# Attention with a soft mixture of experts on one core: whole PSUM tiles for the products with v and the dispatch, ordered readers, and four sets of due numbers

## The chip, the cores and the metric

The kernel runs on one core of one Trainium2 chip. The metric is the device time of one execution in microseconds. The kernel before was timed in three runs: median 568.11 us, from 567.79 to 571.41. The profile is of a further execution.

## What is computed

Everything is float32. There are 8 batches with 8 heads, 576 tokens and a head size of 64. The first half is attention in which only the scores within tau of the row's maximum count; its result, with the heads of a token joined to 512 numbers, goes into a soft mixture of 8 experts with 4 slots each.

```python
scores = q @ k.T / 8
scores = where(scores >= max(scores) - tau, scores, -1e9)
attn = softmax(scores)                     # over the keys
x = join_heads(attn @ v)                   # 4608 x 512
logits = x @ phi                           # 4608 x 32
d = softmax(logits, axis=0)                # dispatch: over all tokens
slot_in = d.T @ x                          # 32 x 512
slot_out[e] = relu(slot_in[e] @ w1[e]) @ w2[e]
out = softmax(logits, axis=1) @ slot_out   # combine: over the slots
```

## The kernel before

**Pairs.** The work goes in 32 pairs of heads, four to a batch (`pair(p)`, L449; `j` is the pair's place in its batch, 0 to 3). The two heads of a pair lie on the two halves of the 128 partitions. A pair has nine row tiles `i` of 128 queries (the ninth holds the 64 queries left over of each head). Per row tile:
- TensorE multiplies q by k (`qk`, L494; the matmuls are L497, those of the ninth tile L502) into a PSUM tile;
- VectorE copies the negated scores to SBUF (`ss`) and takes the row's extreme in the same instruction (`nmx`, L509);
- ScalarE makes the exponentials `p` (L519), GpSimd the threshold `thr` (L522);
- VectorE masks `p` by the threshold and sums the row (L525).

After two row tiles TensorE transposes their `p` by 64 x 64 blocks (`ptr`, L418, matmuls at L424) and ScalarE copies the result out of PSUM (`act_copy`, L428, copies at L429) to `pTa` (the first 256 queries of a head), `pTb` (the other 320) or `pTl` (the left-over keys). For the ninth tile, the left-over rows `pL` are transposed at once with some left-over keys, and four copies read that one PSUM tile: one to `pTl`, one of 512 elements to `pTb` (L594), two of 64 partitions to `pTl` (L597). In the last pair the copy to `pTb` runs on VectorE (L433), else on ScalarE.

When the pair's rows are there, two products with v follow (L601 to L616; matmuls L612): 20 matmuls over `pTa` for 256 queries, 20 over `pTb` for 320, each into a PSUM tile of its own and copied to `xT`. Then `xT` is transposed to `x`; GpSimd scales `x` by the reciprocal sums (L627), and TensorE and ScalarE turn it back to `xT` (L632, L635; the operations called "new" in the plan).

**The dispatch.** After the fourth pair of a batch, `dispatch(b)` (L669) transposes the left-over columns (`xl`), multiplies `xT` by phi into the tile `wl` (the logits, L690), which then has three readers: VectorE's reduction to `M` (L695), ScalarE's exponential `dT` (L702), which needs the running extreme that a second small reduction makes of `M` (L698), and ScalarE's copy `l` of the logits for later (L429). `f` (L700) is the factor by which the sums so far are rescaled. `dT` and `l` are transposed; then `weigh` (L730) sums `ones` and `x` with the weights into `csum` and `acc` (L737 and L742, taken over by VectorE at L748 or L750). After the eighth batch ("end") the same runs with nothing beside it, followed by the slots' input.

**PSUM.** PSUM is four tiles of 128 x 2 x 512 float32, called regions (L31, L269). A buffer of kind "s" takes a whole region. A buffer of kind "w" takes one of its two halves of 512: a half of a region that is half used if there is one, else of an empty region (`take`, L185). Of kind "w" are the products with v, the logits and the two results of `weigh`, except in the last pair and the last batch, and three small uses at the start and the end:

```python
bank_of = lambda alone: Buf("s" if alone else "w")          # L412
w = bank_of(p == NP - 1)                                    # L604, products with v
wl = bank_of(b == B - 1)                                    # L684, logits
w = bank_of(b == B - 1)                                     # L733, weigh
```

**The order of the work.** Operations are not issued as they are written: each is added to a plan (`Order.add`, L135) with its engine, an assumed duration, what it reads and writes, and a due number. The due number is the pair's base (9 per pair) and an entry of `TABLE` (L41) under the operation's scope and its place in it: "first" and "last" for those pairs, "pair" for the 30 others, "batch" and "end" for the dispatches, "new", "soft" and so on. `plan` (L160) plays the operations through with the assumed durations: whenever an engine is free it takes, among its operations whose inputs are there and whose buffers have room, the one with the smallest due number. The order that comes out, and the buffers given, are then written down for each engine as they stand (`run`, L265); the waits between engines are put in when the kernel is built, from the tiles that the instructions touch. Loads by SyncE are in the plan too. In `add`, an operation depends on the writers of what it reads, and on the writers and the readers of what it writes (L144 to L148); two that only read the same thing are not ordered.

After the last batch come the experts and the combine (L870 to L1040), in an order written by hand, with eight PSUM tiles of their own.

## Time and profile before

| | us |
|---|---|
| median of three runs | 568.11 |
| lowest, highest run | 567.79, 571.41 |
| the profiled execution's own time | 567.51 |
| its span, first to last instruction | 565.7 |
| TensorE busy | 535.9 |
| VectorE busy | 468.8 |
| ScalarE busy | 458.0 |
| GpSimd busy | 251.6 |

The mean granted TensorE clock was 0.988 of full speed. In the profile, PE is TensorE's matmuls, PEld its weight loads, DVE is VectorE, ACT ScalarE, POOL GpSimd, SP SyncE. A row of the timeline gives the start, the length, the engine, the line, the operation, output and inputs, and a count where neighbours are merged; in square brackets stands how long the engine had been idle, and whose end released it. A row of waits names who waited for whom, with the total, the times and the longest. In a name such as `ps` the number of the buffer is left out, so the four regions are all `ps`. A line of the kernel can be a helper's: all transposes by `ptr` are L424 and all of ScalarE's copies by `act_copy` L429. Matmuls are pipelined and their ends are modelled.

### The profile page before, as it was taken

To read this page: it belongs to the slowest core of one execution; us is meant where nothing else is said; L and a number is where in the kernel's file an instruction comes from. 1 tells how busy PE (TensorE), PEld (TensorE's weight loads), DVE (VectorE), ACT (ScalarE), POOL (GpSimd) and SP (SyncE) were. 2 spreads that over 40 slices of the span, in tenths; PEclk is the share of its full clock that TensorE was granted. 3 is DMA by queue.
4 is the path that set the end of the run, shared out by engine and by line. 5 is a ranking of instruction groups with operands and counts; after the bars stand their busy time and mean duration, and the time that the engine had idled before them with its cause. 6 is when DMAs were issued, how large, how long until landed. Compare 5 with 4: busy or idle time off the path is not lost.

```text
span 565.7 us, 18326 instructions
## 1 busy us (share of the span) xinstructions
PE 535.9 (95%) x7022; PEld 346.4 (61%) x7022; DVE 468.8 (83%) x1327; ACT 458.0 (81%) x789; POOL 251.6 (44%) x478
## 2 busy tenths in 40 slices
PE   8999999999899999999899989998999998899991
PEld 6666666666566665666566656665666665553470
DVE  6999997999699979998899979996999899321192
ACT  4899998999799979999799979997999799412171
POOL 2465553555355544555355525553555556221030
PEclk9999999999999999999999999999999999899996
DMA  6255555555555552333033313333333413979488
GB/s 176 66 162 163 162 170 153 163 162 162 161 159 164 164 163 73 101 83 94 16 94 105 93 46 89 87 89 87 89 87 88 126 61 94 370 286 404 190 346 322
DMA packets 31990, 83.03 MB, mean 147 GB/s; under 512 B 4640, under 2 KB 12832, under 8 KB 31904
## 3 DMA queue, kind: packets, MB, share of 16 engines
q1 hardware_dynamic: 31904, 81.87, 46.8%
q8 instruction: 55, 0.90, 0.7%
q14 instruction: 31, 0.25, 0.1%
HBM read 72.42 MB, written 9.44 MB: 145 GB/s over the span
## 4 chain that ended last, share of the span: by engine, by line
PE 71%; ACT 17%; DVE 5%; issue 4%; SPq 1%; DMA 0%; DVEq 0%; POOL 0%; ACTq 0%; POOLq 0%
PE ps L612 25%; PE ps L497 19%; PE ps L424 14%; ACT p L519 6%; ACT pTa L429 3%; PE h L914 2%; PE ps L502 2%; ACT pTb L429 2%; PE so L948 2%; PE ps L632 1%; PE ps L737 1%; DVE ss L509 1%; ACT xT L429 1%; DVE cT L906 1%; ACT pL L519 1%
## 5 line engine op out<-in xcount | busy, mean ns | idle before, releaser
L509 DVE TENSOR_SCALAR_CACHE_REDUCE ss<-ps 128x576 f32<-128x576 f32 x288 | 208.0, 754 | 12.5 <-ACT pTl L429 8.9
L522 POOL TENSOR_SCALAR thr<-nmx,pabs 128x1 f32<-128x1 f32 x288 | 120.5, 419 | 199.7 <-DVE ss L509 190.1
L525 DVE SCALAR_TENSOR_TENSOR p<-ss,thr,p 128x576 f32<-128x576 f32 x256 | 201.4, 811 | 9.5 <-ACT p L519 9.0
L519 ACT ACTIVATE p<-ss,nmx 128x576 f32<-128x576 f32 x256 | 186.5, 778 | 18.9 <-DVE ss L509 18.7
L497 PE MATMUL ps<-k,q 64*128 64x288 f32 x1024 | 165.9, 427 | 6.4 <-ACT xT L429 4.9
L497 PEld LDWEIGHTS ps<-k,q 64*128 64x128 f32 x1024 | 85.0, 188 | 32.5 <-ACT pTb L429 14.0
L424 PE MATMUL ps<-ident,p 64*128 64x64 f32 x2304 | 100.8, 225 | 2.8 <-ACT pTa L429 1.5
L424 PEld LDWEIGHTS ps<-ident,p 64*128 64x128 f32 x2304 | 87.5, 140 | 19.1 <-ACT pTa L429 6.4
L429 ACT COPY pTb<-ps 128x1024 f32<-128x1024 f32 (+1 forms) x95 | 79.9, 872 | 2.3 <-PE ps L424 1.5
L612 PE MATMUL ps<-pTb,vv 128*64 128x320 f32 x512 | 75.9, 438 | 0.1
L429 ACT COPY pTa<-ps 128x1024 f32<-128x1024 f32 x64 | 65.7, 1028 | 0.4 <-PE ps L424 0.4
L612 PE MATMUL ps<-pTa,vv 128*64 128x256 f32 x512 | 62.9, 388 | 0.0
L612 PEld LDWEIGHTS ps<-pTb,vv 128*64 128x64 f32 x512 | 34.0, 136 | 36.0 <-issue 10.0
L612 PEld LDWEIGHTS ps<-pTa,vv 128*64 128x64 f32 x512 | 34.2, 138 | 26.1 <-DVE ss L509 9.0
L556 POOL TENSOR_SCALAR pL<-pL,ri 128x576 f32<-128x576 f32 x31 | 34.9, 1126 | 27.7 <-DVE ri L552 25.6
L612 PE MATMUL ps<-pTl,vv 128*64 128x256 f32 (+1 forms) x256 | 41.9, 406 | 0.0
L627 POOL TENSOR_TENSOR x<-x,ri 128x512 f32<-128x512 f32 x31 | 33.2, 1072 | 1.6 <-ACT x L429 1.6
L429 ACT COPY pTl<-ps 128x256 f32<-128x256 f32 x64 | 24.0, 376 | 5.2 <-PE ps L424 3.0
L429 ACT COPY xT<-ps 128x256 f32<-128x256 f32 (+1 forms) x63 | 24.6, 390 | 3.1 <-PE ps L612 3.1
L525 DVE SCALAR_TENSOR_TENSOR pL<-ss,thr,pL 128x576 f32<-128x576 f32 x32 | 26.5, 828 | 0.0
L879 POOL TENSOR_TENSOR c<-lall,crow 128x512 f32<-128x512 f32 x9 | 9.3, 1043 | 38.7 <-PE ct L416 38.7
L612 PEld LDWEIGHTS ps<-pTl,vv 128*64 128x64 f32 x256 | 18.4, 137 | 12.7
(137 smaller groups left out, 561.7 us busy)
## 6 DMA issues: line engine op xcount, KB each, us to landing
w<-in_w SPq DMA_DIRECT2D x44, 512.0 KB, 7.0
q<-in_qT SPq DMA_DIRECT2D x62, 288.0 KB, 4.5
vv<-in_vt SPq DMA_DIRECT2D x32, 320.0 KB, 4.6
host<-in_w SPq DMA_DIRECT2D x20, 512.0 KB, 6.7
k<-in_kT SPq DMA_DIRECT2D x62, 144.0 KB, 3.0
out<-w SPq DMA_DIRECT2D x8, 512.0 KB, 3.3
out<-host SPq DMA_DIRECT2D x8, 512.0 KB, 5.0
out<-host SPq DMA_DIRECT2D x4, 256.0 KB, 4.6
```

What stands on the lines that cost most here:

```text
L424: nc.tensor.transpose(out=s[:, g, c:c + 64], in_=ins[g], identity=ident[rows[g], rows[g]], tile_position=(64 * g, 0))
L429: G.add("ACT", 51 + 0.833 * n, nom, lambda: nc.scalar.copy(*io()), r, w)
L497: nc.tensor.matmul(s.t[:, g, 0:HS], qt.t[rows[g], h, c * 128:(c + 1) * 128], kt.t[rows[g], h * HS:(h + 1) * HS], start=True, stop=True, ti ...
L502: nc.tensor.matmul(s.t[rows[a], g, 0:HS], qt.t[rows[g], a, SM:S], kt.t[rows[g], a * HS:(a + 1) * HS], start=True, stop=True, tile_position ...
L509: dve(674, t + OFF['mx'], [s], [ss, nmx], lambda s=s, ss=ss, nmx=nmx: nc.vector.tensor_scalar(out=ss.t.rearrange("p (a k) -> p a k", a=2), ...
L519: G.add("ACT", 668, t + OFF['ex'], lambda sv=sv, nmx=nmx, view=view: nc.scalar.activation(view().rearrange("p (a k) -> p a k", a=2), sv(), ...
L522: pool(250, t + OFF['th'], lambda nmx=nmx, thr=thr: nc.gpsimd.tensor_scalar(out=thr.t, in0=nmx.t, scalar1=1.0, scalar2=pabs, op0=ALU.mult, ...
L525: fn=lambda sv=sv, thr=thr, view=view, i=i: nc.vector.scalar_tensor_tensor(out=view().rearrange("p (a k) -> p a k", a=2), in0=sv(), scalar ...
L556: pool(725, t + OFF['sc'], lambda k=k, view=view_: nc.gpsimd.tensor_scalar(out=view(), in0=view(), scalar1=ri.t[:, k:k + 1], **one), [ri[c ...
L612: nc.tensor.matmul(lone(w)[h * 64:(h + 1) * 64, 0:n], vv.t[:, v0:v0 + 64], p0, start=(kb == 0), stop=(kb == 4), tile_position=(0, h * 64), ...
L627: G.add("POOL", 1040, u + 6.8, own="new", r=[ri[0]], w=[x[j]], fn=lambda: nc.gpsimd.tensor_tensor(out=wide(), in0=wide(), in1=ri.t[:, 0:8] ...
L914: nc.tensor.matmul(hp[n][g * 32:(g + 1) * 32, :], siT[:, kb, :], t[g][:, n * 512:(n + 1) * 512], start=(kb == 0), stop=(kb == 3), tile_pos ...
```

## The change

`bank_of` now always gives a whole region: the products with v, the logits and the results of `weigh` no longer share a region with another buffer. Halves are left for the three small uses.

`Order.add` makes a reader of a PSUM tile depend on earlier-added readers of it on other engines. The plan also keeps, for each region, when each engine was last done with a half of it, and starts an operation on a half only when all other engines are done with that region (`clear`, `half`).

The copy of 512 elements into `pTb` in the last pair runs on ScalarE, as in the other pairs.

The due numbers are new throughout. The sets "pair" and "new" are replaced by one set for each place in the batch, "pair0" to "pair3" and "new0" to "new3". In the sets of a pair the numbers between 140 and 200 are those of TensorE's operations, in the order in which they are added.

No matmul, activation or copy is added or taken away, and no size changes. The diff, with the tables cut to the sets spoken of:

```diff
@@ TABLE @@
...
-    ("pair", [
-        -72.29, -65.52, -44.15, 856.12, -44.14, 158.19, 483.24, 1464.37, 843.77, 568.47, 160.78, 452.32, 1365.83, 860.12,
-        625.58, None, None, None, None, 166.25, 1437.38, 158.45, 487.24, 1412.63, 844.02, 630.13, 158.45, 542.26,
-        1373.37, 844.01, 614.53, None, None, None, None, 166.79, 1446.33, 153.65, 1502.81, 163.84, 632.71, 1511.14,
-        843.78, 659.56, 166.38, 457.56, 1429.66, 865.11, 689.61, None, None, None, None, 169.68, 1364.17, 163.14,
-        446.59, 1445.40, 857.44, 659.57, 166.37, 670.40, 1356.40, 858.43, 506.20, 863.63, 615.21, None, None, 172.38,
-        1388.49, 163.51, 434.83, 1502.82, 883.39, 476.55, 874.12, 606.20, 843.80, 170.60, 1364.15, 1446.06, 1418.97, 1413.83,
-        170.45, 1355.16, 175.43, 1429.67, 182.21, 1362.06,
-    ]),
+    ("pair0", [
+        -208.85, -167.24, -157.01, 1001.41, -214.44, 166.18, 510.28, 1532.00, 1036.12, 470.56, 165.98, 516.54, 1528.42, 1062.86,
+        448.79, None, None, None, None, 169.45, 1503.60, 167.65, 502.87, 1551.89, 1008.86, 510.00, 166.82, 496.26,
+        1482.23, 1001.42, 471.52, None, None, None, None, 157.11, 1529.00, 151.03, 1522.29, 169.46, 413.78, 1533.40,
+        990.77, 493.67, 165.59, 511.89, 1498.95, 1008.79, 500.52, None, None, None, None, 159.20, 1528.08, 168.85,
+        422.42, 1507.96, 990.78, 495.52, 168.86, 471.53, 1490.72, 1001.61, 511.76, 1018.18, 457.80, None, None, 175.18,
+        1498.94, 167.53, 513.33, 1484.10, 1028.69, 488.00, 1026.04, 516.53, 1006.14, 148.92, 1513.99, 1512.25, 1544.74, 1533.88,
+        173.84, 1522.15, 177.48, 1553.75, 187.44, 1489.74,
+    ]),
+    ("pair1", [
+        -208.69, -170.64, -138.71, 1071.08, -200.78, 164.47, 563.73, 1128.63, 1032.08, 533.07, 164.02, 535.08, 1105.19, 1013.19,
+        599.51, None, None, None, None, 167.88, 1090.07, 164.83, 626.91, 1122.71, 1038.29, 520.66, 164.42, 569.84,
+        1104.05, 1019.80, 666.92, None, None, None, None, 160.98, 1153.18, 168.44, 1142.51, 167.87, 664.30, 1087.18,
+        1037.84, 492.41, 164.22, 578.83, 1125.22, 1070.65, 667.56, None, None, None, None, 175.95, 1258.94, 168.32,
+        630.47, 1274.82, 1064.18, 667.50, 166.96, 622.99, 1105.11, 1019.35, 678.13, 1027.58, 664.29, None, None, 177.33,
+        1096.19, 166.97, 650.57, 1120.88, 1071.07, 562.18, 1023.62, 522.94, 1022.18, 168.20, 1119.64, 1104.65, 1251.86, 1134.55,
+        163.54, 1120.90, 180.20, 1082.33, 189.88, 1120.89,
+    ]),
+    ("pair2", [
+        -201.21, -159.15, -130.02, 865.17, -122.78, 162.94, 326.97, 1727.51, 817.90, 316.43, 160.22, 369.78, 1747.74, 844.54,
+        396.90, None, None, None, None, 169.73, 1764.42, 162.00, 326.98, 1702.83, 836.84, 353.27, 158.11, 358.28,
+        1693.51, 791.64, 369.00, None, None, None, None, 172.13, 1756.75, 169.92, 1801.50, 169.99, 350.71, 1653.71,
+        816.06, 380.95, 170.02, 356.24, 1761.99, 806.60, 360.76, None, None, None, None, 174.84, 1761.76, 168.34,
+        341.09, 1709.30, 867.64, 377.45, 167.67, 342.13, 1854.72, 804.42, 351.79, 891.94, 401.15, None, None, 177.76,
+        1746.03, 169.12, 359.10, 1753.28, 839.24, 401.16, 817.17, 342.12, 817.89, 177.28, 1750.00, 1722.19, 1875.96, 1789.18,
+        176.77, 1746.60, 182.62, 1663.79, 186.60, 1702.84,
+    ]),
+    ("pair3", [
+        -202.48, -166.29, -145.39, 337.53, -196.08, 163.91, 790.74, 1583.13, 336.16, 799.95, 165.23, 779.23, 1484.30, 356.54,
+        786.56, None, None, None, None, 172.12, 1562.22, 166.55, 786.88, 1589.69, 339.42, 792.55, 165.41, 817.96,
+        1571.68, 348.97, 823.69, None, None, None, None, 173.97, 1573.56, 172.62, 1598.60, 170.72, 794.52, 1563.85,
+        368.26, 805.82, 171.97, 777.55, 1468.05, 383.51, 793.92, None, None, None, None, 166.56, 1553.23, 168.28,
+        797.19, 1587.40, 392.53, 797.23, 173.19, 774.81, 1579.34, 374.52, 791.51, 377.07, 778.00, None, None, 176.41,
+        1621.85, 169.83, 781.53, 1470.41, 389.80, 795.53, 336.17, 807.50, 379.68, 167.72, 1484.30, 1484.31, 1607.68, 1582.66,
+        176.58, 1590.98, 179.58, 1458.28, 184.68, 1576.85,
+    ]),
...
@@ -143,6 +179,8 @@
         deps = set(after)
         for x in r:
             deps.update(self.hits(self.writers, x))
+            if x[0].kind in ("s", "w"):
+                deps.update(j for j in self.hits(self.readers, x) if self.ops[j][0] != eng)
         for x in w:
             deps.update(self.hits(self.writers, x))
             deps.update(self.hits(self.readers, x))
@@ -174,6 +212,10 @@
         slot = {}
 
         region = [set() for _ in range(REGIONS)]
+        last = [{} for _ in range(REGIONS)]
+
+        def clear(g, eng):
+            return max((v + CROSS.get((e, eng), LAT[e]) for e, v in last[g].items() if e != eng), default=0.0)
 
         def room(k):
             if k == "s":
@@ -182,13 +224,17 @@
                 return sum(2 - len(u) for u in region if 2 not in u)
             return len(free[k])
 
+        def half(t):
+            fit = [g for g, u in enumerate(region) if 2 not in u and len(u) < 2 and clear(g, "PE") <= t]
+            return max(fit, key=lambda g: len(region[g])) if fit else None
+
         def take(k):
             if k not in "sw":
                 return free[k].pop(0)
             if k == "s":
                 g, i = next(g for g, u in enumerate(region) if not u), 2
             else:
-                g = max((g for g, u in enumerate(region) if 2 not in u and len(u) < 2), key=lambda g: len(region[g]))
+                g = half(t)
                 i = 1 if 0 in region[g] else 0
             region[g].add(i)
             return (g, i)
@@ -228,7 +274,15 @@
                 while q:
                     x = heapq.heappop(q)
                     need = [b.kind for b in ops[x[1]][4] if b.kind is not None and b not in slot]
-                    if all(room(k) >= need.count(k) for k in need):
+                    ok = all(room(k) >= need.count(k) for k in need)
+                    if ok:
+                        late = [clear(slot[b][0], eng) for b in ops[x[1]][4] if b.kind == "w" and b in slot]
+                        if "w" in need and half(t) is None:
+                            late.append(min(clear(g, "PE") for g, u in enumerate(region) if 2 not in u and len(u) < 2))
+                        if max(late, default=0.0) > t:
+                            heapq.heappush(ev, (max(late), 2, -1))
+                            ok = False
+                    if ok:
                         got = x[1]
                         break
                     skip.append(x)
@@ -251,6 +305,9 @@
                     end += SWITCH * (o[5] != mode) + 50 * (engfree[eng] < t)
                     mode = o[5]
                 engfree[eng] = end
+                for b in o[4]:
+                    if b.kind == "w":
+                        last[slot[b][0]][eng] = end + (o[6] if eng == "PE" else 0)
                 heapq.heappush(ev, (end, 2, -1))
                 heapq.heappush(ev, (end + LAT[eng] + o[6], 0, got))
                 for j in succ[got]:
@@ -409,7 +466,7 @@
     rows = [slice(0, 64), slice(64, 128)]
 
 
-    bank_of = lambda alone: Buf("s" if alone else "w")
+    bank_of = lambda alone: Buf("s")
     lone = lambda w: w.t[:, 0] if w.kind == "s" else w.t
 
     def tr(o, i):
@@ -450,7 +507,7 @@
         b, j = divmod(p, HP)
         t0 = p * N9
         late = p == NP - 1
-        G.scope("first" if p == 0 else "last" if p == NP - 1 else "pair", t0)
+        G.scope("first" if p == 0 else "last" if p == NP - 1 else f"pair{j}", t0)
         kt, qt, vv = (Buf(k) for k in ("k", "q", "vv"))
         last[:] = kt, qt, vv
         pTa, pTb, pTl, pL, r, ri = (Buf(k) for k in ("pTa", "pTb", "pTl", "pL", "r", "ri"))
@@ -591,7 +648,7 @@
                     (w.t, k * 64, [pL.t[rows[g], g * SL + k * 128:][:, 0:128] for g in range(2)]) for k in range(4)] + [
                     (w.t, 256, [pL.t[rows[0], S - 128:S], pL.t[rows[1], 0:128]])] + left_keys(2, 320, w))
                 act_copy(256, t + OFF['te'], [w], [pTl[2]], lambda w=w: left_out(2, 320, w))
-                copy(p == NP - 1, 512, t + OFF['te'], [w], [pTb["L"]], lambda w=w: (
+                act_copy(512, t + OFF['te'], [w], [pTb["L"]], lambda w=w: (
                     pTb.t[:, :, :, SM - QA:S - QA], w.t[:, :, 0:256].rearrange("p g (k q) -> p g k q", k=4)))
                 for g in range(2):
                     G.add("ACT", 225, t + OFF['te'], lambda w=w, g=g: nc.scalar.copy(
@@ -624,15 +681,15 @@
         if not late:
             xj = lambda: x.t[:, :, j * 128:(j + 1) * 128]
             wide = lambda: xj().rearrange("p c (h d) -> p c h d", h=2)
-            G.add("POOL", 1040, u + 6.8, own="new", r=[ri[0]], w=[x[j]], fn=lambda: nc.gpsimd.tensor_tensor(
+            G.add("POOL", 1040, u + 6.8, own=f"new{j}", r=[ri[0]], w=[x[j]], fn=lambda: nc.gpsimd.tensor_tensor(
                 out=wide(), in0=wide(), in1=ri.t[:, 0:8].rearrange("p (c h) -> p c h", h=2).unsqueeze(3).to_broadcast(
                     [128, 4, 2, 64]), op=ALU.mult))
             w = Buf("s")
-            G.add("PE", 248, u + 7, own="new", r=[x[j]], w=[w], fn=lambda w=w: [
+            G.add("PE", 248, u + 7, own=f"new{j}", r=[x[j]], w=[w], fn=lambda w=w: [
                 nc.tensor.transpose(out=w.t[:, g, c * 64:c * 64 + 64], in_=xj()[rows[g], c],
                                     identity=ident[rows[g], rows[g]], tile_position=(64 * g, 0))
                 for c in range(4) for g in range(2)])
-            G.add("ACT", 477, u + 7.3, own="new", r=[w], w=[xT[0], xT[1]], fn=lambda w=w: nc.scalar.copy(
+            G.add("ACT", 477, u + 7.3, own=f"new{j}", r=[w], w=[xT[0], xT[1]], fn=lambda w=w: nc.scalar.copy(
                 xT.t[:, 0:SM].rearrange("p (c g q) -> p g c q", c=4, g=2),
                 w.t[:, :, 0:256].rearrange("p g (c q) -> p g c q", c=4)))
 
```

More of the change, by code (lines that the diff above doesn't have):

```diff
@@ L41 @@
     ("first", [
[7 rows of a table removed]
-    ]),
-    ("pair", [
[7 rows of a table removed]
[7 rows of a table added]
     ]),
     ("last", [
[7 rows of a table removed]
[7 rows of a table added]
     ]),
     ("end", [
-        320.58, 412.37, 518.01, 612.55, 641.57, 409.69, 458.90, 437.78, 501.31, 412.68, 343.67, 416.62, 656.76, 332.77,
-        659.56, 629.94, 432.43, 644.77, 483.70, 676.80, 488.19, 625.38, 657.32, 418.56, 483.71, 630.33, 486.47, 612.54,
-        326.81, 480.08, 653.82,
+        635.02, 222.30, 635.03, 884.35, 786.79, 194.11, 221.66, 209.51, 492.40, 213.82, 653.01, 233.76, 801.84, 524.02,
+        811.00, 884.36, 248.25, 903.87, 542.06, 811.02, 658.66, 811.01, 811.01, 227.55, 666.83, 796.50, 632.21, 881.94,
+        491.74, 653.02, 786.80,
     ]),
     ("soft", [
-        193.82, 250.85, -171.20, 174.48, 192.31, 196.12,
+        27.63, 27.62, -312.54, 26.80, 28.26, -7.62,
     ]),
     ("batch", [
-        -35.96, 173.40, -18.94, -847.48, -836.99, 183.61, 180.42, 191.40, -35.97, 205.43, -45.34, 174.12, -847.49, -35.97,
-        -871.12, -43.12, -816.87,
-    ]),
-    ("new", [
-        1652.84, -326.45, -371.73,
+        -62.11, -152.03, -63.33, -1010.94, -1010.93, -130.22, -93.56, -111.14, -36.34, -160.31, -58.44, -111.55, -1032.75, -27.29,
+        -1039.18, -45.27, -1014.49,
+    ]),
+    ("new0", [
+        1831.60, -166.33, -276.91,
+    ]),
+    ("new1", [
+        1608.61, 22.81, -920.27,
+    ]),
+    ("new2", [
+        1255.54, -750.92, -123.71,
+    ]),
+    ("new3", [
+        1682.14, -780.86, -618.82,
+    ]),
[8 rows of a table added]
+    ]),
[8 rows of a table added]
+    ]),
[8 rows of a table added]
+    ]),
[8 rows of a table added]
     ]),
```

28 rows, old and new, of the table TABLE are left out of this document.

## Prediction

> **What bounds the kernel now.** I read the shares and slices of the page first, then the busy time of each engine over single pairs of heads, then the waits, and last the instructions in order of time around one place.
>
> ```profile
> span 565.7 us, 18326 instructions
> PE 535.9 (95%) x7022; PEld 346.4 (61%) x7022; DVE 468.8 (83%) x1327; ACT 458.0 (81%) x789; POOL 251.6 (44%) x478
> DVE  6999997999699979998899979996999899321192
> PE 71%; ACT 17%; DVE 5%; issue 4%; SPq 1%; DMA 0%; DVEq 0%; POOL 0%; ACTq 0%; POOLq 0%
> ```
>
> TensorE is nearly always busy, and the chain that ended last runs on it for 71%. In the slices DVE dips at regular places (7, 6, 7): once in each batch. The windows below cut the middle of the run at the start of each pair's second product with v: an ordinary pair, the pair at the end of a batch, and an ordinary one of the next.
>
> ```profile
> 187.34:200.90 13.56, 13.56 (x180) 8.96 (x182) 13.20 (x39) 13.11 (x23) 7.12 (x15) 1.00 0.56 169
> 200.90:220.21 19.31, 17.74 (x286) 11.35 (x288) 14.85 (x44) 15.30 (x29) 6.79 (x15) 1.00 0.40 120
> 233.77:247.32 13.55, 13.55 (x180) 8.93 (x182) 13.18 (x39) 13.11 (x23) 7.40 (x15) 1.00 0.35 91
> ```
>
> Columns after the length: busy time of PE, PE's weight loads, DVE, ACT, POOL; granted clock; DMA. An ordinary pair is full: PE 13.55 of 13.55 us, DVE 13.2, ACT 13.1. Nothing can be saved there but PE work. A pair that carries a batch's dispatch takes 19.3 us, and in it PE idles 1.57 us, DVE 4.5, ACT 4.0. Who was waited for, from 28 to 449 us (total, times, longest):
>
> ```profile
> ACT dT L702 <- PE ps L612: 13.0, 5, 2.6
> DVE M L695 <- ACT l L429: 10.1, 7, 1.5
> PEld ps L612 <- issue: 12.3, 32, 0.4
> PE ps L497 <- ACT xT L429: 4.6, 5, 0.9
> PE ps L424 <- ACT dT L702: 2.6, 5, 0.5
> PEld ps L424 <- DVE csum L750: 2.0, 5, 0.4
> ```
>
> Five times ACT stands 2.6 us before dT (the exponential of the dispatch logits) until a PE group of L612 ends, a product with v. By data dT needs only the logits and M. In order of time (start, length, engine), at the third of these batch ends:
>
> ```profile
> 205.47 1.53 PE L690 MATMUL ps<-xT,phi_sb 128*32 128x128 f32 x64
> ...
> 207.44 0.32 ACT L429 COPY l<-ps 128x192 f32<-128x192 f32 x1
> 207.79 0.36 DVE L695 TENSOR_REDUCE M<-ps 128x1 f32<-128x192 f32 x1 [1.46 <-ACT l L429]
> ...
> 209.03 0.14 DVE L698 TENSOR_REDUCE M<-M 128x1 f32<-128x2 f32 x1
> ...
> 210.40 0.60 PE L612 MATMUL ps<-pTl,vv 128*64 128x256 f32 x4
> ...
> 211.04 0.42 ACT L702 ACTIVATE dT<-ps,M 128x192 f32<-128x192 f32 x1 [2.59 <-PE ps L612]
> 211.36 0.28 ACT L700 ACTIVATE f<-M,M 128x1 f32<-128x1 f32 x1
> 211.52 0.34 PE L424 MATMUL ps<-ident,dT 64*128 64x64 f32 x4 [0.52 <-ACT dT L702]
> ...
> 212.88 0.35 ACT L429 COPY xT<-ps 128x256 f32<-128x256 f32 x1
> ...
> 213.29 0.76 PE L497 MATMUL ps<-k,q 64*128 64x288 f32 x4 [0.93 <-ACT xT L429]
> ```
>
> M is ready at 209.17, dT starts at 211.04, 0.04 after the product's last matmul ends (210.40 + 0.60). Both read or write a half ("w") of a two-bank tile, and I read the wait as theirs being halves of one tile, ordered as a whole. What is late next is the copy of xT behind dT in ACT's queue, and behind that the q k product that wants the tile: PE idles 0.52 + 0.93 = 1.45 us. The reduction of M is the second wait: it starts 0.03 after ACT's copy of the same logits ends (207.44 + 0.32), though it reads another way and writes something else. Two readers of one tile on two engines run one after the other here, in the order of the plan.
>
> The first batch end has no such stall, with the same work but for f and one small M reduction, and is a measure of what it costs:
>
> ```profile
> 89.97 0.42 ACT L702 ACTIVATE dT<-ps,M 128x192 f32<-128x192 f32 x1 [0.42 <-DVE M L695]
> ...
> 91.75 1.95 PE L612 MATMUL ps<-pTa,vv 128*64 128x256 f32 x16
> ...
> 75.54:106.66 31.12, 30.95 (x464) 20.30 (x466) 27.77 (x81) 28.25 (x50) 15.05 (x29) 1.00 0.49 145
> 193.75:226.62 32.87, 31.30 (x465) 20.27 (x466) 28.11 (x82) 28.41 (x51) 13.97 (x29) 1.00 0.46 139
> ```
>
> There the product starts after dT. From first product to first product two pairs on, it takes 31.12 us against 32.87: 1.75 less.
>
> **The change, part by part.** *Whole tiles.* Each product with v and each dispatch product takes a whole two-bank tile, so dT's wait for a neighbour's product has no cause left. Worth per batch end: 1.45 by PE's own bubbles, 1.75 by the first batch; since that one also lacks f (0.28 on ACT) and the 0.14 us reduction, the truth lies between, and I take 1.6. Batches 2 to 6: 5 x 1.6 = 8.0. The seventh, where dT also waits, has smaller bubbles:
>
> ```profile
> 451.40 0.42 ACT L702 ACTIVATE dT<-ps,M 128x192 f32<-128x192 f32 x1 [2.59 <-PE ps L612]
> 451.87 0.34 PE L424 MATMUL ps<-ident,dT 64*128 64x64 f32 x4 [0.52 <-ACT dT L702]
> 452.98 0.76 PE L497 MATMUL ps<-k,q 64*128 64x288 f32 x4 [0.27 <-ACT xT L429]
> ```
>
> 0.52 + 0.27 = 0.8. The eighth used whole tiles already. Gain 8.8.
>
> The Trainium skill (PSUM — Partial Sum Buffer, "PSUM bank collisions raise a hardware error") says that engines collide only in the same bank and quadrant and need ordering only there, and its "Terms" give a bank 2 KiB per partition, which is one half of such a tile. By that rule dT never had to wait for the other half; if the program orders by bank, the wait has another cause and the sum is no gain at all, while by the row the wait is there whatever its need. That is the rival "nothing removed" below.
>
> *What whole tiles cost.* There are four. A half goes to a half-used tile if one is there, else to an empty one, so it costs more only when two halves are open together. In an ordinary pair they never are:
>
> ```profile
> 187.34 2.84 PE ps L612 x20
> ...
> 193.75 2.31 PE ps L612 x20
> 203.78 0.43 ACT L429 COPY xT<-ps 128x320 f32<-128x320 f32 x1
> ```
>
> The first product ends at 190.18, its copy is a matter of 0.43 us, the second starts at 193.75. So ordinary pairs pay nothing unless the order moves the two together. At a batch end the logits, a product with v and the two weighing products (csum, acc) can be open at once and take up to two tiles more. Bounds: nothing, if dT frees the logits' tile some 2 us earlier as I expect, to one more wait like PE's weight load for csum, 0.41 us (2.0 over 5), at seven batch ends, 2.9. I take 0, because the logits' tile is held for less long.
>
> *Ordered readers.* The plan now runs M's reduction before the copy l. At batches 1 to 7 that lies beside the above (DVE was idle there, 1.46 us) and brings M about 0.35 earlier, l 0.36 later; l's transposes wait on PE, which has q k products to put ahead. After the last batch nothing hides it:
>
> ```profile
> 494.29 0.32 ACT L429 COPY l<-ps 128x192 f32<-128x192 f32 x1 [0.55 <-PE ps L690]
> 494.64 0.36 DVE L695 TENSOR_REDUCE M<-ps 128x1 f32<-128x192 f32 x1 [2.74 <-ACT l L429]
> ```
>
> The reduction can start where the copy did: 0.35 gained.
>
> *The last pair's copy into pTb* goes from DVE to ACT, 512 elements:
>
> ```profile
> 485.74 0.69 DVE L433 COPY pTb<-ps 128x512 f32<-128x512 f32 x1 [1.96 <-PE ps L424]
> 486.85 0.42 ACT L597 COPY pTl<-ps 64x64 f32<-64x64 f32 x2
> ...
> 488.43 2.32 PE L612 MATMUL ps<-pTb,vv 128*64 128x320 f32 x16
> L429 ACT COPY pTb<-ps 128x512 f32<-128x512 f32 x4 | 2.3, 585 | 0.1
> ```
>
> ACT is done at 487.27, with this copy at 487.86, before the product that needs it at 488.43: it hides behind the product of L612 that runs until then. Without that cover it costs up to 0.59.
>
> *Four sets of order parameters.* No instruction comes or goes; due numbers change, those of SP's loads and POOL's too, but loads still go as their tiles come free. The PE numbers of a pair lie between 153.65 and 182.21 before and between 148.92 and 189.88 after, so TensorE's order within a pair should stay much as it is. Bounds: a product group more or less between operations of another array mode in an ordinary pair, priced by the gap in weight loads before L612, 12.3 / 32 = 0.38 us, in three pairs of seven batches, 8.0 either way. I take 0. The first and the last pair, each with a new set of its own, have bubbles that an order can close or double; the largest is
>
> ```profile
> 481.26 1.05 PE L424 MATMUL ps<-ident,p 64*128 64x64 f32 x20 [1.47 <-ACT pTa L429]
> ```
>
> so I allow 1.5 us either way.
>
> Sum against the profiled execution, 567.51 us (its span 565.7 and 1.8 around it): 567.5 - 8.8 - 0.35 = 558.4. The median of the runs is 0.6 above that execution: **559.0 us**. Own range: most gain 6 x 1.75 + 0.35 = 10.9, least 5 x 1.45 + 0.8 - 2.9 = 5.2, with 1.5 us for the end pairs: 555.7 to 564.4.
>
> **The rivals.**
> *The orders save PE work too* (faster): an ordinary pair loses one change of array mode, 559.0 - 8.0 = 551. For: the weight loads idle 0.38 us at each. Against: PE's due numbers hardly move.
> *The tile is still awaited*: dT comes early, but the q k product goes on waiting 0.93 for a tile, now since all four are taken. Then only 0.52 comes back at six batch ends, 3.1, and 0.35: 568.1 - 3.5 = 564.6. For: that wait names the copy which frees a tile. Against: the first batch end has none of it.
> *Nothing removed*: dT waits on the product for another reason, which the trace doesn't name. 567.8 with the end's 0.35. Against: the first batch's dT, planned ahead of the product, waited for M alone.
> *Tiles run short* (slower): the place is the q k product behind each product with v, which now holds a tile of two banks until its copy; if the new orders bring two of them together, two tiles are left for nine q k products and DVE, 97% busy, starves. The price is a wait like 0.38 us at two products in 28 pairs, 21 us, less 9.15: 580. It decides from 9.15 / 56 = 0.16 us per product. Against: in ordinary pairs each product already takes an empty tile.
> The Trainium skill (Perfetto Trace Analysis, "Optimization Strategy") reads one gap that repeats on the engine that should be full as a sign of too little PSUM; the 0.93 us gap, five times alike, fits that, and by it a change that leaves fewer tiles lengthens the gap instead of closing it.
>
> **How the numbers follow.** Forecast 0.63; PE work saved 0.10; tile still awaited 0.10; nothing removed 0.07; tiles short 0.10. A measurement of this kernel tells about 1%, 5.7 us, from no change. Of the forecast 0.04 falls inside 1%. Faster by over 1%: 0.59 + 0.10 = 0.69; within 1%: 0.04 + 0.10 + 0.07 = 0.21; slower: 0.10. The range reaches from the first rival, 551, past the second to 566 and leaves out the two others and half the first, about 0.2.
>
> **What would show it.** Right: no wait of dT on L612; PE's idle 0.52 and 0.93 gone; M's reduction ahead of the copy l at all eight batches; batches 2 to 6 at about 58.4 us instead of 60; ordinary pairs still 13.55 us. Wrong: ordinary pairs longer than 13.7 (tiles short) or under 13.3 (PE work saved); new PE waits for copies at batch ends; a start or an end longer by more than 1.5 us.

## The result, and the profile after

| | before | after |
|---|---|---|
| median of the runs of this comparison, us | 569.72 (567.79 to 571.41, 4 runs) | 554.45 (553.82 to 555.40, 4 runs) |
| profiled execution, us | 567.51 | 553.97 |
| its span, us | 565.7 | 552.2 |

The ratio of the runs is 0.9734, with a 95% interval of 0.969 to 0.9779: the kernel is 2.7% faster. Forecast were 559.0 us and a gain of 9.2; the gain is 13.5 between the two profiled executions and 15.3 between the medians. 554.45 lies 1.3 us below the range that the sum gave itself (555.7 to 564.4), and inside the wider one of the chances (551 to 566). On the page of after, line numbers are 57 higher (L747 is the logits, L752 and L755 the reductions to M, L759 dT, L669 the products with v, L486 ScalarE's copies, L481 the transposes). Its span, busy times, DVE's slices and the chain:

```profile
span 552.2 us, 18305 instructions
PE 530.8 (96%) x7022; PEld 340.9 (62%) x7022; DVE 470.6 (85%) x1326; ACT 458.6 (83%) x790; POOL 247.5 (45%) x478
DVE  6999998999999998999999989998999999212192
PE 88%; DVE 4%; ACT 3%; issue 2%; POOL 1%; DVEq 0%; POOLq 0%; ACTq 0%
```

The dips of DVE at the batch ends are gone (all 8 or 9 until the last pair), and the chain runs on TensorE for 88% of the span instead of 71%; ScalarE's part fell from 17% to 3%. Three pairs in windows cut at each pair's second product with v, as in the prediction; the third carries the dispatch:

```profile
171.34:184.89 13.55, 13.53 (x180) 8.86 (x182) 12.87 (x39) 13.17 (x23) 7.19 (x15) 1.00 0.55 169
184.89:198.94 14.05, 14.05 (x184) 9.05 (x186) 13.73 (x41) 13.65 (x24) 7.26 (x15) 1.00 0.54 163
198.94:215.51 16.57, 16.57 (x282) 10.68 (x284) 14.98 (x44) 14.77 (x28) 7.47 (x15) 1.00 0.46 140
```

The pair with the dispatch takes 16.57 us instead of 19.31, and PE is busy in all of it. The ordinary pair ahead of it is 0.5 longer (184 matmuls instead of 180, where the pair with the dispatch now has 282 instead of 286), so the batch is what to compare: two and a quarter us in both pairs together. From here on a batch is measured from the start of its logits to the start of the next ones. For the second batch, before and then after:

```profile
145.50:205.47 59.97, 58.40 (x822) 38.14 (x818) 54.65 (x158) 54.64 (x95) 28.95 (x57) 1.00 0.49 148
```

```profile
145.54:203.26 57.72, 57.70 (x820) 37.51 (x818) 54.81 (x157) 54.58 (x95) 29.04 (x57) 1.00 0.52 158
```

2.25 us less. Over the span the 13.5 us lie so: the first logits start at 87.26 before and at 87.91 after (+0.65); the six batches from the first logits to the seventh take 358.57 and 346.25 (-12.3; the first of them gives 0.6, the others 2.25 to 2.46); from the seventh logits to the eighth, with the last pair, 46.86 and 45.26 (-1.6); from there to the experts 9.94 and 9.69 (-0.25); what follows is the same 63.1. So nine tenths of the gain lie in these batches, as forecast, but the ends of batches 2 to 6 gave 2.3 to 2.5 where 1.6 was allowed, and that of the first 0.6 where nothing was. The order in time at the third batch end of after:

```profile
203.26 1.53 PE L747 MATMUL ps<-xT,phi_sb 128*32 128x128 f32 x64
...
204.86 0.36 DVE L752 TENSOR_REDUCE M<-ps 128x1 f32<-128x192 f32 x1
205.03 0.70 PE L554 MATMUL ps<-k,q 64*128 64x288 f32 x4
...
205.66 1.95 PE L669 MATMUL ps<-pTa,vv 128*64 128x256 f32 x16
206.30 0.32 ACT L486 COPY l<-ps 128x192 f32<-128x192 f32 x1
206.52 0.43 ACT L759 ACTIVATE dT<-ps,M 128x192 f32<-128x192 f32 x1
...
207.44 0.60 PE L669 MATMUL ps<-pTl,vv 128*64 128x256 f32 x4
207.97 0.34 PE L481 MATMUL ps<-ident,l 64*128 64x64 f32 x4
...
208.14 0.29 PE L481 MATMUL ps<-ident,dT 64*128 64x64 f32 x4
```

No row of these has a bracket: none of these instructions waits. M starts 0.07 after the logits' modelled end, before the copy l; dT runs beside the product with v and is done at 206.95, a microsecond before the transposes that need it. And the order on TensorE is another one: between the logits and the product with v stand only eight transposes of xT and one q k group (the product starts 2.4 us after the logits), and the transposes of l and dT come behind the product. Before, the transposes of l and a second q k group came first, and the product 3.15 us after the logits' start (208.62 below).

**What the idle column had left out.** The forecast's lower price of a batch end, 1.45 us, is the idle time in the brackets. Matmul ends are modelled, though, and a row's modelled end can lie over a wait. From start to start it is seen. Before, in an ordinary pair, and then at the third batch end:

```profile
196.48 0.70 PE L497 MATMUL ps<-k,q 64*128 64x288 f32 x4
197.02 0.66 PE L424 MATMUL ps<-ident,p 64*128 64x64 f32 x16
...
199.16 0.71 PE L424 MATMUL ps<-ident,p 64*128 64x64 f32 x16
199.71 0.46 PE L497 MATMUL ps<-k,q 64*128 64x288 f32 x2
...
206.93 0.76 PE L497 MATMUL ps<-k,q 64*128 64x288 f32 x4
...
207.81 0.34 PE L424 MATMUL ps<-ident,l 64*128 64x64 f32 x4
...
208.62 1.95 PE L612 MATMUL ps<-pTa,vv 128*64 128x256 f32 x16
...
211.69 0.67 PE L424 MATMUL ps<-ident,p 64*128 64x64 f32 x16
```

Four q k matmuls ahead of transposes take 0.54 (196.48 to 197.02) and at the batch end 0.88: 0.34 of waiting for the copy l, with no bracket. Sixteen transposes ahead of q k take 0.55, at the batch end 1.60 (211.69 to the q k at 213.29 in the prediction): 1.05 instead of 0.93. And the part of the product over pTl, 0.53 in the rows of after above (207.44 to 207.97), took 1.12 ahead of dT's transposes (210.40 to 211.52): 0.59 instead of 0.52. Together 1.98 us, of the 2.29 by which the batch with this end, the third, became shorter (59.98 to 57.69). The other 0.3 is not traced.

### The profile page after: what moved, and what is told of

Same layout as the page of the kernel before. It is cut to its first block, busy times and chain, and to the rows that moved or that the text cites. A ratio compares the mean times of both kernels' runs of the same rounds, so it can differ in the third digit from the quotient of the medians.

```text
span 552.2 us, 18305 instructions
## 1 busy us (share of the span) xinstructions
PE 530.8 (96%) x7022; PEld 340.9 (62%) x7022; DVE 470.6 (85%) x1326; ACT 458.6 (83%) x790; POOL 247.5 (45%) x478
## 4 chain that ended last, share of the span: by engine, by line
PE 88%; DVE 4%; ACT 3%; issue 2%; POOL 1%; DVEq 0%; POOLq 0%; ACTq 0%
PE ps L669 29%; PE ps L554 24%; PE ps L481 17%; PE ps L559 3%; PE h L971 3%; PE so L1005 2%; PE ps L689 2%; PE ps L747 2%; PE ps L473 2%; PE ps L794 1%; DVE p L582 1%; PE up L421 1%; ACT pTa L486 1%; DVE ss L566 1%; DVE host L1057 1%
## 5 line engine op out<-in xcount | busy, mean ns | idle before, releaser
L579 POOL TENSOR_SCALAR thr<-nmx,pabs 128x1 f32<-128x1 f32 x288 | 132.0, 460 | 179.2 <-DVE ss L566 159.6
L481 PE MATMUL ps<-ident,p 64*128 64x64 f32 x2304 | 99.0, 225 | 3.5 <-ACT pTa L486 2.1
L481 PEld LDWEIGHTS ps<-ident,p 64*128 64x128 f32 x2304 | 88.4, 139 | 20.7 <-ACT pTa L486 3.8
L554 PEld LDWEIGHTS ps<-k,q 64*128 64x128 f32 x1024 | 83.3, 188 | 21.8 <-ACT pTl L654 5.8
L486 ACT COPY pTb<-ps 128x1024 f32<-128x1024 f32 (+1 forms) x96 | 83.7, 873 | 5.1 <-PE ps L481 2.9
L669 PE MATMUL ps<-pTb,vv 128*64 128x320 f32 x512 | 75.9, 438 | 0.0
L486 ACT COPY pTa<-ps 128x1024 f32<-128x1024 f32 x64 | 64.9, 1017 | 0.4 <-PE ps L481 0.4
L669 PE MATMUL ps<-pTa,vv 128*64 128x256 f32 x512 | 62.9, 388 | 0.0
L669 PEld LDWEIGHTS ps<-pTb,vv 128*64 128x64 f32 x512 | 33.9, 136 | 36.3 <-issue 8.5
L669 PEld LDWEIGHTS ps<-pTa,vv 128*64 128x64 f32 x512 | 34.2, 138 | 26.6 <-DVE ss L566 8.5
L669 PE MATMUL ps<-pTl,vv 128*64 128x256 f32 (+1 forms) x256 | 41.9, 406 | 0.0
L486 ACT COPY xT<-ps 128x256 f32<-128x256 f32 (+1 forms) x63 | 25.0, 397 | 7.0 <-PE ps L669 6.0
L669 PEld LDWEIGHTS ps<-pTl,vv 128*64 128x64 f32 x256 | 18.4, 137 | 12.7
L576 ACT ACTIVATE pL<-ss,nmx 128x576 f32<-128x576 f32 x32 | 24.8, 775 | 0.4 <-DVE ss L566 0.4
L534 POOL TENSOR_SCALAR k<-k,flag 128x576 f32<-128x576 f32 x31 | 24.0, 775 | 1.3 <-DMA k<-in_kT 1.0
```

Of the source, the lines that this page charges most:

```text
L481: nc.tensor.transpose(out=s[:, g, c:c + 64], in_=ins[g], identity=ident[rows[g], rows[g]], tile_position=(64 * g, 0))
L486: G.add("ACT", 51 + 0.833 * n, nom, lambda: nc.scalar.copy(*io()), r, w)
L534: sc = lambda e, kc=kc: lambda: e.tensor_scalar(out=kt.t[:, kc], in0=kt.t[:, kc], scalar1=flag8, **one)
L554: nc.tensor.matmul(s.t[:, g, 0:HS], qt.t[rows[g], h, c * 128:(c + 1) * 128], kt.t[rows[g], h * HS:(h + 1) * HS], start=True, stop=True, ti ...
L576: G.add("ACT", 668, t + OFF['ex'], lambda sv=sv, nmx=nmx, view=view: nc.scalar.activation(view().rearrange("p (a k) -> p a k", a=2), sv(), ...
L579: pool(250, t + OFF['th'], lambda nmx=nmx, thr=thr: nc.gpsimd.tensor_scalar(out=thr.t, in0=nmx.t, scalar1=1.0, scalar2=pabs, op0=ALU.mult, ...
```

## The experiments

All are one change taken apart: the tiles, the rule for readers, the due numbers. A batch below is that from the second logits to the third; "the end" is from the seventh logits to the eighth (46.86 before, 45.26 after). Ratios are to the kernel before, run on the same chip.

**1. Whole tiles alone.**

```diff
-    bank_of = lambda alone: Buf("s" if alone else "w")
+    bank_of = lambda alone: Buf("s")
```

> The kernel before with one edit: every product with v and every dispatch product takes a whole tile; due numbers and the rest as before. If dT waited because its tile was shared with a product with v, the wait of dT on that product is gone at batch ends 2 to 7 and the batches 2 to 6 take about as long as the first batch end shows, 58.2 us instead of 60.0: some 10 us less in all, 557 to 560. The rest of the 13.5 us of the whole change is then the order's. If the new due numbers carry the gain and the tiles do nothing by themselves, it stays within 3 us of the kernel before.

Measured: 567.91 us, ratio 0.9955 (0.9924 to 0.9986), span 565.8. The batch, and two rows of the waits from 28 to 449 us:

```profile
145.49:204.62 59.13, 58.52 (x823) 38.37 (x819) 54.70 (x158) 54.62 (x95) 29.77 (x57) 1.00 0.51 154
```

```profile
DVE M L695 <- ACT l L429: 10.2, 7, 1.5
ACT dT L702 <- DVE M L698: 4.9, 6, 0.9
```

dT no longer waits for the product with v: that wait did come from the halves. But the batch is only 0.84 us shorter, not 1.6. dT now waits for M, as M still waits for the copy l; and the plan, given other tiles, moved the product with v behind dT's transposes, 5.23 us after the logits' start. At the end 5.1 us are lost (52.00), so that hardly anything is left of the whole.

**2. The rule for readers alone.**

```diff
             deps.update(self.hits(self.writers, x))
+            if x[0].kind in ("s", "w"):
+                deps.update(j for j in self.hits(self.readers, x) if self.ops[j][0] != eng)
```

> The kernel before with one edit: readers of a tile on different engines are ordered in the plan as they are added; halves and due numbers as before. If sharing is the cause, dT still waits for the product with v and the time falls by 0 to 2 us (0.35 at the end, and up to 0.34 at each batch end where the transposes of l waited for the copy of l). If the order of the readers is the cause, because M is ready sooner and dT comes ahead of the product, 8 us or more are gained.

Measured: 571.12 us, ratio 1.0009 (0.9978 to 1.0039), span 569.3. Its batch, and dT's wait:

```profile
145.72:205.34 59.62, 58.17 (x823) 38.40 (x819) 54.60 (x158) 54.67 (x95) 28.92 (x57) 1.00 0.51 152
```

```profile
ACT dT L704 <- PE ps L614: 10.2, 5, 2.0
```

M goes ahead of l, a batch gains 0.35, and dT still waits for the product, 2.0 instead of 2.6. The end is 5.8 longer.

**3. Both, with the old due numbers.**

> The kernel before with both edits, whole tiles and ordered readers, and still the old due numbers for all pairs. If the two edits are the change and the due numbers nothing, it comes to 554 to 556. If the four sets bring 2 to 3 us of their own, it stays at 556 to 559.

Measured: 563.08 us, ratio 0.9869 (0.9816 to 0.9921), span 560.8.

```profile
145.51:204.28 58.77, 58.09 (x822) 38.44 (x818) 54.61 (x158) 54.68 (x95) 29.33 (x57) 1.00 0.51 155
```

TensorE's longest waits from 28 to 449 us, and the third batch end:

```profile
PE ps L426 <- ACT dT L704: 4.1, 6, 0.7
```

```profile
207.78 0.34 PE L426 MATMUL ps<-ident,dT 64*128 64x64 f32 x4 [0.68 <-ACT dT L704]
...
209.13 1.95 PE L614 MATMUL ps<-pTa,vv 128*64 128x256 f32 x16
```

It is slower than both values expected. Within a batch the two add up: 0.84 + 0.35 = 1.19, measured 1.20; the end is 49.14. What remains is that PE waits 0.7 for dT, six times; here the transposes of l and dT come ahead of the product with v, which starts 4.85 us after the logits (204.28). After is 1.05 us a batch below this, and has the same tiles and the same rule: that part belongs to the due numbers.

**4. A whole tile for the logits alone**, in the kernel before:

```diff
-        wl = bank_of(b == B - 1)
+        wl = Buf("s")
```

> The kernel before with one edit: the logits alone take a whole tile, the products with v and the two weighing products keep halves. If the neighbour of the logits is all that counts, the time is that of whole tiles for all, within 1.5 us. If the weighing products' sharing (the wait for csum, up to 0.41 us at a batch end) counts too, it is 1.5 to 3 us slower than whole tiles for all.

Measured: 571.65 us, ratio 1.0032 (0.9997 to 1.0066), span 569.2; a batch takes 59.82. dT is free of the product here too (it waits for M, 4.9 us in 6 times), yet the batch is 0.7 longer than with whole tiles for all, and the run 3.7, where at most 3 was expected: now the products with v and the results of weigh still share regions, VectorE waits 4.5 us in 5 times to take over `acc` and ScalarE 5.4 us in 5 times to copy xT, all for TensorE at L742. The halves hurt wherever two of them were open together.

**5. The halves put back into after** (the edit of 1 the other way round, all else as in after).

> The changed kernel with one part undone: products with v, logits and weighing products take halves again, with the new due numbers, ordered readers and the plan's knowledge of shared tiles. A product with v and the logits share a tile again. If the due numbers and the knowledge are what counts (dT is now placed behind the product anyway), it stays within 2 us of the changed kernel, 554 to 556.5. If whole tiles are needed under any order, dT and then TensorE wait again and it loses 0.9 us or more a batch, 560 or above.

Measured: 566.88 us, ratio 0.9949 (0.9929 to 0.997), span 563.4. Its batch, and two rows at the third batch end:

```profile
146.53:205.29 58.76, 58.00 (x820) 37.88 (x818) 54.96 (x157) 54.64 (x95) 29.49 (x57) 1.00 0.52 156
```

```profile
207.69 1.95 PE L669 MATMUL ps<-pTa,vv 128*64 128x256 f32 x16
...
210.11 0.32 ACT L486 COPY l<-ps 128x192 f32<-128x192 f32 x1 [0.24 <-PE ps L669]
```

1.04 us a batch. The product starts early, as in after, and the copy l and dT, which share its region, come only when it ends: 2.42 us from the product's start to l, against 0.64 in after. TensorE then waits for what follows from dT, the copy d ahead of `weigh` (3.8 us in 7 times), for which no matmul of after waits. The end is 5.1 longer as well (50.33).

**6. The rule for readers taken out of after.**

> The changed kernel without the rule that orders two readers of a tile; all else as in it. At the batch ends TensorE's order comes out the same, so if the due numbers already put M's reduction ahead of the copy l there, the time stays within 2 us, 553 to 556.5, and what is lost is lost at the end, where the reduction then may come behind the copy (0.35). If the rule is what brings M early, some 0.4 us a batch are lost, 557 or above.

Measured: 554.98 us, ratio 0.9747 (0.9718 to 0.9776); a batch takes 57.76, as in after. Only after the last batch does the order of the two readers change, and there it costs. This kernel, then after:

```profile
482.37 0.32 ACT L484 COPY l<-ps 128x192 f32<-128x192 f32 x1 [0.55 <-PE ps L745]
482.72 0.36 DVE L750 TENSOR_REDUCE M<-ps 128x1 f32<-128x192 f32 x1 [2.74 <-ACT l L484]
```

```profile
481.08 0.36 DVE L752 TENSOR_REDUCE M<-ps 128x1 f32<-128x192 f32 x1 [2.46 <-PE ps L747]
...
481.48 0.32 ACT L486 COPY l<-ps 128x192 f32<-128x192 f32 x1 [1.01 <-DVE M L752]
```

From the logits' start to dT's transposes it is 3.34 us without the rule (480.77 to 484.11) and 3.07 with it: 0.27, where 0.35 was forecast. In the batches the new due numbers put M first without it.

**7. One old set for all pairs**: after with "pair" and "new" in their old form in place of the eight sets, the other numbers new.

```diff
-        G.scope("first" if p == 0 else "last" if p == NP - 1 else f"pair{j}", t0)
+        G.scope("first" if p == 0 else "last" if p == NP - 1 else "pair", t0)
```

> The changed kernel with the old single set of due numbers for all pairs between first and last, and the old set for the operations called new; the new sets for first and last pair, batch and end. If four sets, one for each place in the batch, bring the last 1.0 us a batch, it loses 5 to 7 us, 559 to 562. If the new numbers of batch, last and end bring it, it stays within 2 us of the changed kernel.

Measured: 563.25 us, ratio 0.9887 (0.9852 to 0.9922), span 562.9.

```profile
148.12:206.68 58.56, 58.09 (x821) 38.38 (x819) 54.46 (x157) 54.65 (x95) 29.49 (x57) 1.00 0.52 157
```

0.84 us a batch is due to the sets of the pairs, and the end is 49.08. The product with v comes 6.35 us after the logits' start here (2.4 in after), and the transposes of l and dT ahead of it. Only 0.24 us of it is waiting for dT: the sixteen transposes ahead of l's take 0.79 (209.46 to 210.25, 0.04 after dT ends) instead of 0.55. Another 0.45 goes by ahead of a q k product that VectorE releases:

```profile
211.05 0.76 PE L518 MATMUL ps<-k,q 64*128 64x288 f32 x4 [0.33 <-DVE ss L530]
```

**8. dT's transposes later**: kernel 3, with the ninth number of "batch" (dT's transposes) raised from -35.97 to 182.

> Whole tiles and ordered readers with the old due numbers, and one number changed: the transposes of dT get 182 in place of -36, which in the plan puts them behind the product with v and three more groups. In the kernel with the two edits alone TensorE stands 0.7 us before these transposes at each batch end, since dT is not there yet. If that place is what the old numbers have wrong, this comes back: 0.7 us in six or seven batches, 557.5 to 559.5. If the stall only moves (acc and csum come later and their reader too), it stays at 562 to 564.

Measured: 570.11 us, ratio 1.0009 (0.9992 to 1.0027), span 568.5: not what was expected. The batch, and the place where PE waits now:

```profile
145.64:205.05 59.41, 58.45 (x823) 38.49 (x819) 55.53 (x158) 54.95 (x95) 30.51 (x57) 1.00 0.51 154
```

```profile
208.54 0.72 PE L425 MATMUL ps<-ident,p 64*128 64x64 f32 x16 [0.68 <-ACT dT L703]
```

dT's transposes are out of the way, and the next group, the transposes of p, waits 0.68 for dT instead. It uses nothing of dT, so what it wants is most likely the tile that the logits hold until dT has read it. A group that is moved away doesn't close a stall if the one behind it waits for the same instruction. That the batch became 0.64 longer than in 3 is explained only in part: a wait of up to 0.3 us for the copy into `pTa` came with it, in five batches. The end is 53.14.

**9. The product with v behind the transposes of l and dT**: after, and one move in the finished order at the first seven batch ends.

```diff
-        for i in sorted(range(len(start)), key=lambda i: (start[i], i)):
+        seq = sorted(range(len(start)), key=lambda i: (start[i], i))
+        for d in self.turned[:-1]:              # d: transposes of dT
+            k = seq.index(d)
+            m = next(n for n in range(k, -1, -1) if self.ops[seq[n]][0] == "PE" and self.ops[seq[n]][5] == COLS)
+            seq.insert(k, seq.pop(m))
+        for i in seq:
```

> The changed kernel with the same plan and the same tiles, and one swap in the order that comes out of it: at the first seven batch ends the product with v that follows the logits is issued behind the transposes of l and dT in place of ahead of them. If the new order gains because this product (2.31 us of TensorE work) covers the way from the logits over M to dT, TensorE now waits some 1.1 us at each batch end (dT ends 1.3 us after the place where the product began, less 0.3 of the two transposes): batches of 58.8 us, 561 to 563 in all. If the gain of the new numbers comes from elsewhere in the pairs, the swap costs under 0.3 us a batch, 554 to 556.5.

Measured: 579.52 us, ratio 1.0158 (1.009 to 1.0227), span 578.8. From the second batch end on, ScalarE's copy of xT stands ahead of the moved product in the order and copies what the tile held before, so these batches' x is not the product with v and TensorE waits for that copy too. Only the first batch end shows the move by itself:

```profile
91.56 0.34 PE L487 MATMUL ps<-ident,dT 64*128 64x64 f32 x4 [0.95 <-ACT l L492]
```

```profile
88.14:146.93 58.79, 57.81 (x821) 37.49 (x819) 54.53 (x156) 54.37 (x94) 28.82 (x57) 1.00 0.52 157
```

PE waits 0.95 with nothing to do, and the batch behind it takes 58.79 against 57.63 in after: 1.16 us for the place of one product. The other batches take 62 to 63 us: two waits each, and what the clock makes of them (last section).

**10. The old sets "last", "end" and "soft" in after.**

> The changed kernel with the old sets of due numbers for the last pair, the end and the row softmax between them; all others new. The batches before the last pair stay at 57.7 us. If the end needs numbers made for the order that runs into it, as the four mixed kernels hint (49 to 53 us from the last but one logits to the last, against 46.9 before and 45.3 after the change), it loses 3 to 7 us, 557.5 to 561.5. If the last pair takes either set alike, it stays within 1.5 us of the changed kernel.

Measured: 556.41 us (554.04 to 559.34), ratio 0.9754 (0.9695 to 0.9813). A batch is as in after (57.70), the end 47.94, in an execution of 559.34. Most of what was expected did not come: by the medians the new sets at the end are worth 1.9 us against the control below, and the two intervals overlap. The four executions took 554.04, 554.20, 558.62 and 559.34 us at granted clocks of 0.990, 0.991, 0.985 and 0.982, so the old sets reach the control's time where the clock holds.

**11. Real durations for the planner**: after, with the assumed durations of M, of the small M, of f and of dT (269, 69, 200, 250 ns) set to the profile's (358, 142, 283, 420).

> The changed kernel with four assumed durations of the dispatch set to those of the trace (M's reduction 358 for 269 ns, the small reduction 142 for 69, f 283 for 200, dT 420 for 250); the order hardly changes: at the batch ends x's product and csum's swap tiles, and the end's filling transposes shift. If the plan's error no longer matters once the product covers dT, no difference over 0.3 us. If tiles at the batch end are tight, the swap of tiles costs or brings 0.1 to 0.3 us a batch, up to 2 us.

Measured: 554.48 us, ratio 0.972 (0.9679 to 0.976). No difference from the control: these four are not what limits the order.

**12. After once more, as a control** beside 9, 10 and 11.

> The changed kernel itself, on the same chip as the three others, as their measure: 553.8 to 555.4.

Measured: 554.53 us, ratio 0.9721 (0.9681 to 0.9762), profiled span 553.9. No version tried is faster than after beyond the intervals.

## Why the prediction was right in direction and too small

The sum had 9.2 us for tiles and readers and nothing for the due numbers. Kernel 3 is that sum, and its span is only 4.9 us shorter than before; the rest of the change, the due numbers above all, brings the other 8.6 (560.8 to 552.2). That the total came as near as it did is luck in part: a term put at nothing made up for one that was too large.

- **dT's wait for the neighbouring half**: right. It went with the whole tiles (1) and the sharing came back with the halves (5). The Trainium skill (PSUM — Partial Sum Buffer, "PSUM bank collisions raise a hardware error") has software order engines by bank and quadrant, two readers on different engines included. The runs agree for the readers: M and l read the same part of the same tile and never overlap, in either order (0.03 to 0.04 us between them). For the two halves no order would be needed by that rule; the program had one all the same, and dropping the sharing dropped it. "Nothing removed" fell.
- **"Whole tiles: I take 1.6"** was mis-sized twice, in opposite directions. The batch end as a whole held 2.25 to 2.46 us, not 1.45 to 1.75: the bracketed idle time left out waits that lie under modelled ends. The benchmark of 1.75 from the first batch end suffered from the same fault, as that place was not free of waits: after shortened its batch by 0.6 too, and four of its q k matmuls ahead of l's transposes took 0.88 (88.72 to 89.60), like the ones above. But whole tiles by themselves gave only 0.84 of it, as behind dT's first wait stood M's, and behind that the place of the transposes.
- **"Four sets of order parameters: I take 0"** is the step that failed. I argued that TensorE's numbers hardly move, so its order hardly moves. It did: with whole tiles and the old numbers of the pairs the product with v stands behind the transposes of l and dT, 4.85 to 6.35 us after the logits' start (1, 3, 7), with the new numbers ahead of them, at 2.4. There its 2.3 us are what TensorE does while f, l and dT are made. The due numbers are worth 1.05 us a batch in all (after against 3), just under half of the gain. That the product's place is a cause of its own is shown at the first batch end alone (9): moved back, TensorE waits 0.95 ahead of dT's transposes and the batch is 1.16 longer. The old sets of the pairs cost 0.84 (7), but there TensorE waits only 0.24 for dT and 0.45 for VectorE, so the cover is not all that the new sets bring. Whether four sets are needed, or one well-made set would do, was not tried.
- **Ordered readers**: 0.35 a batch, but only with the old numbers (2, 3); nothing with the new ones (6). 0.27 at the end, forecast 0.35.
- **The tiles' cost, taken as 0**: right. With four tiles and no halves no new wait of more than 0.3 us for a tile appeared in after; "tiles run short" fell, though one ordinary pair passed its sign of 13.7 us (14.05), for the four matmuls that it took over. That "the tile is still awaited" fell for after, but its mechanism is most likely the stall of 8.
- **PE work saved**: its time, 551, is nearer to the measured one than the forecast is, but its mechanism fell. Two of the three ordinary pairs take 13.55 to 13.6 us as before, and 1.98 of the 2.29 us at the third batch end are waits.
- **The copy into pTb**: hidden, as forecast. In the last pair the product over pTb follows 2.82 us after the one over pTa, against 2.80 before.
- **First and last pair, 1.5 either way**: the first lost 0.65 (the same program started its first logits 0.5 later still in 12). The 1.6 gained between the last two logits hold the seventh batch end too, for which 0.8 was forecast: up to the next product over pTb it gave 0.83 (14.11 to 13.28, and 18 matmuls more in it), so the last pair by itself gained 0.8 at most.

The edits do not add up over the whole run. Alone they are worth 0.45%, 0 and 0 (1, 2, 4), together 2.7%: each moved the stall to the next wait, and with the old numbers each lengthened the last pair by 2 to 6 us. Part of that is the clock's doing, and the traces bound it (below).

## What to carry to other kernels

Price a stall by the starts of TensorE's groups against the same groups elsewhere, not by the idle column, and ask for each wait removed which one ends just behind it: here three stood in a row (the neighbour's product, the other reader, the place of the transposes), and a single edit gave a third of the sum. To cover a chain over three engines, put behind its first link the longest TensorE group that needs neither its result nor its tile. A change of resources pays in full only with an order made for it, so try the parts together with the order as well as alone.

## What the runs showed of the hardware

The granted TensorE clock falls to half for stretches of 3.41 us or multiples after idle times that are short by themselves. In kernel 9, after the second batch end (columns as before; the clock is the third figure from the right):

```profile
148.58:151.99 3.41, 1.27 (x20) 0.68 (x18) 2.86 (x8) 3.36 (x8) 1.66 (x4) 1.00 0.97 340
151.99:155.40 3.41, 3.15 (x16) 1.83 (x18) 1.08 (x5) 0.65 (x3) 0.00 (x0) 0.50 0.09 32
155.40:158.81 3.41, 3.41 (x62) 1.95 (x58) 0.94 (x3) 1.93 (x5) 0.27 (x1) 1.00 0.00 0
```

```profile
150.66 0.34 PE L487 MATMUL ps<-ident,l 64*128 64x64 f32 x4 [1.27 <-ACT dT L765]
...
152.25 3.48 PE L675 MATMUL ps<-pTa,vv 128*64 128x256 f32 x16 [1.12 <-ACT xT L492]
```

Two waits, 1.27 and 1.12 us, and the same sixteen matmuls take 3.48 instead of 1.95 us. The two waits and half of 3.41 us make 4.1, and the batch is 4.2 longer than in after. The drops at this kernel's later batch ends and in its last pair (213.43, 278.28, 339.72, 401.16, 496.73) lie on one grid of 3.413 us with this one. In every profile the same happens in the last pair, where TensorE has too little to do; kernel 1, and then after:

```profile
472.78:476.20 3.42, 1.67 (x32) 0.93 (x25) 3.15 (x9) 3.37 (x6) 3.42 (x6) 1.00 0.53 125
476.20:479.61 3.41, 1.23 (x19) 1.03 (x18) 1.71 (x6) 1.14 (x3) 3.41 (x4) 0.50 0.68 229
479.61:483.03 3.42, 2.15 (x24) 1.58 (x26) 2.96 (x9) 2.92 (x4) 1.36 (x4) 0.50 0.84 253
483.03:486.44 3.41, 3.41 (x18) 1.64 (x14) 0.00 (x0) 0.00 (x0) 0.00 (x0) 0.50 0.85 244
```

```profile
466.79:470.20 3.41, 1.48 (x28) 1.10 (x28) 3.41 (x11) 2.29 (x4) 3.01 (x4) 1.00 0.82 258
470.20:473.61 3.41, 3.09 (x38) 2.44 (x38) 0.29 (x1) 3.41 (x6) 0.90 (x1) 0.50 0.94 306
```

Kernel 1 loses three stretches at half the clock there, after one, and so did before (from 483.4). Two stretches more cost at most 3.4 us, which may be most of the 5.1 that kernel 1 loses at the end; at least 1.7 is its order. Kernels 2 and 4 had three stretches as well, 3 two and 8 four, so the clock explains at most 3.4 of their 5.8 and 4.8, 1.7 of 2.3 and 5.1 of 6.3 us. The control, the same program as after, had two stretches and an end of 46.45 us, 1.2 longer. In the windows ahead of the three drops shown, PE was busy 1.27, 1.67 and 1.48 us of 3.41. With each of the fourteen profiles cut into windows of 3.413 us on the grid of its own drops, from 28 to 550 us, every window at full clock with under 1.7 us of PE was followed by one at half, and none with over 2.3; in between are both. A window at half clock was followed by a full one only with 2.9 us of PE or more. The Trainium skill (TensorE: Matmul & The Clock Gate, "What's actually happening") gives a window of 3413 ns and a clock that is either full or half; the traces agree in both. Its table of goals ("Why this matters for your kernels") asks for no idle gap over some 3 us, and here gaps of at most 1.8 us were enough, one to three of them in a window.
